# Two normalisers written with one SBUF operand, and new places for the steps of the attention's units

## The chip, the core and the metric

The kernel runs on one core of a Trainium2 chip. A core has a matrix engine (TensorE, PE in the profile; its weight loads are PEld), a vector engine (VectorE, DVE), a scalar engine (ScalarE, ACT), a general engine (GpSimd, POOL) and an engine that issues DMAs (SyncE, SP). They run side by side and wait for each other by semaphores. SBUF is the working memory, PSUM the eight banks that matrix products are written to. The metric is the time of one execution in device microseconds (us); smaller is better.

## The reference

Four layers on a 2048 x 512 array, each added to its input after a layer norm: Fourier mixing, attention with a compressive memory, and both once more.

```
a, b = x @ dft_hid_re.T, x @ dft_hid_im.T
y    = dft_seq_re @ a - dft_seq_im @ b                 # Fourier layer

for s in range(4):                                     # memory attention: segments of 512 rows, 32 heads of 16
    a_dot = softmax(qs @ ks.T / 4 + mask) @ vs         # causal, within the segment
    a_mem = (phi(qs) @ M) / (phi(qs) @ z + 1e-6)       # memory of the earlier segments
    o     = g * a_mem + (1 - g) * a_dot                # g = sigmoid(beta), one per head
    M, z  = M + phi(ks).T @ vs, z + sum(phi(ks))
out = o @ wo
```

## The kernel before

Everything is one program of four stages: Fourier, attention, Fourier, attention. Each stage consists of small generators (a projection, the scores of four heads, a memory read). A call `place(order, generator, slots)` says in which time slot each next step of a generator is written; at the end all slots are gone through in order of time, and inside a slot in order of the first number. Slots can be fractions; they are places in an order, not times. TensorE executes its matmuls in exactly this order (L118 is the helper that pins them). On the other engines a scheduler of the framework sets the order, apart from pinned instructions, so a step that is written elsewhere also moves its evictions and its DMAs.

An attention stage works through 4 segments x 4 groups of 8 heads x 2 units of 4 heads: 32 units, 10 slots each (`SU`). In the slots around a unit's start t stand:

- `stack` at t + `STK`: SP loads the unit's queries and keys as stacks (`stkq`, `stkk`, 2 DMAs each) from DRAM buffers (`scrq`, `scrk`) into which the projections were stored.
- `natural_max` at t + `N_AT`: scores in natural layout (`nat` banks, of 512, 128+384 and four times 256 columns). DVE takes each row's maximum straight from the bank (L963), and at the end writes the maxima as two-part numbers (`mparts`, L982 and L983).
- `max_rows` at t - 5: TensorE transposes them (`mT`), ACT copies them (`mt`, L998), SP writes them as extra rows into `stkq` (L1001).
- `softmax_values` at t + `S_AT`: transposed scores (`sT`), five pairs of banks: `third`, `second` twice, `first` twice. ACT applies relu on the diagonal blocks (L1034) and the exponential (`pT`, L1037); POOL zeroes what is not causal (L1040). In the last three units of the program DVE does half of the relu (L1032).
- `value_products` at t + `PV`: the products with the values (`pv_bank`, 32 matmul rows in the trace). `output` at t + `TURNED`: four transposes (`on`), the reciprocal of the row sums, times 1 - g (`rec`, L1127 and L1128), and the scaled result (L1144, L1153), which POOL adds to `onat` (L1151).

Between these stand steps that come once a group or a segment, at 2.5 slots (`W`) into a unit whose number a table gives: `mem_read` (`pm`, its normaliser `den` in L1171 to L1173, its result `onat` in L1180; table `READ_AT`), `mem_update` (`pkT`, then `pM`; `UPA` and `UPB`), `prep` (`xnT`; layer norm and transposes of the next segment; `PREP_AT`) and `transpose_out` (`oT`, split into `oh`; `OT_AT`). Every table has a variant for the first or the last segment (`_FIRST`, `_LAST`).

The rest of TensorE's time in a unit goes to a chain of projections (`pqk`, `pvv`) and output projections (`po`). `ORDER` lists 16 tiles a segment, "-" being an empty place. Each tile has 12 steps (4 blocks of 128 rows, 3 passes each); a step does the product on 64 of the 128 rows, and the other half follows `LAGS` steps later, so that two tiles run side by side on the two halves of the array. `WIN` spreads a unit's 24 steps over three stretches of its slots. All banks come from one pool of 8; a chain tile holds its bank for 12 + `LAGS` steps.

The second Fourier stage reads its rows in pairs (`normalise`, `ROWS_AT` in the new text), and its first products (`m`) are mixed into the last units of the first attention. Nothing follows the second attention; its last segment has empty places in `ORDER_LAST`.

Of the kernel before, what the change touches and what calls it, by code (L numbers as in the profile page):

```python
# [15 lines left out]
ALU = mybir.AluOpType  # L16
# [25 lines left out]
VW = DH + 1  # L42
HALF = NT // 2
URGENT = 150
S_AT = (0, 2.5, 3, 6.5, 8)
N_AT = (-17, -15.05, -12, -10.9, -8.0, -8)
PV = 11.5
PVF = 12
W = 2.5
TURN = -5  # L50
TO = 0.8
TURNED = (12.5, 12.5, 14)
WIN = ((4.1, 10), (6.1, 6), (8.1, 8))
LAGS = 17
ORDER = "k3 q3 o1 o0 o2 o3 k0 q0 k1 q1 v0 k2 v1 q2 v3 v2"
OT_AT = (1, 1, 1, 2)
PREP_AT = (2, 3)
READ_AT = (1, 3, 5, 7)
UPA = (0, 3, 5, 7)
UPB = (3, 4, 6, 8)  # L60
ORDER_FIRST = "q3 k3 - - - - v2 k0 q0 k2 k1 q1 v1 q2 v0 v3"
PREP_FIRST = (2, 3)
UPA_FIRST = (1, 3, 4, 7)
UPB_FIRST = (2, 5, 8, 8)
ORDER_LAST = "k3 q3 o2 o3 o0 - - o1 - - - - - - - -"
OT_LAST = (1, 3, 1, 1)
READ_LAST = (1, 3, 5, 5)
S_LAST = (0, 2.5, 3, 6.5, 8)
N_LAST = (-17, -15.05, -13, -11, -8, -8)
PV_LAST = 11.9  # L70
OWO = 0.8
OWU = 0.7
OWP = 0.3
OWR = 0.2
OWB = 0.55
STK = -22
TERMS = {
    "P1": (((0, 1), None, None),),
    "P7": (((1, 1), (0, 1), ALU.add),),
# [12 lines left out]
def spectral_infini_kernel(  # L92
# [649 lines left out]
    def place_attention(x_in, x_out, t0, w_at, out_at):  # L742
# [264 lines left out]
        def softmax_values(s, g, u):  # L1007
            qs, ks = stacks.pop((s, g, u, "q")), stacks.pop((s, g, u, "k"))
            K = KROWS + MROWS
            h0 = g * HG + u * HU  # L1010

            def scores(dst, *cols):
                banks = [bank("sT") for _ in SIDES]
                off, diag = 0, []
                for p, kt in cols:
                    n = 512 - kt * P
                    last = issued[0] + 1
                    for a, at in enumerate(SIDES):
                        T.matmul(
                            banks[a][:, off : off + n],  # L1020
                            ks[at : at + K, p, kt * P : (kt + 1) * P],
                            qs[at : at + K, p, kt * P :],
                            start=True,
                            stop=True,
                        )
                    diag.append(off // P)
                    off += n
                for a, ps in enumerate(banks):
                    blocks = ps.rearrange("p (b c) -> p b c", c=P)
                    blocks = blocks[:, diag[0] : diag[-1] + 1 : max(1, diag[-1] - diag[0])]  # L1030
                    if x_out is out_tiles and (s * NG + g) * NU + u >= NSEG * USEG - 3 and a:
                        V.tensor_scalar_max(blocks, blocks, 0.0)  # L1032
                    else:
                        done = A.activation(blocks, blocks, AF.Relu)  # L1034
                        if a == 0:
                            evicted.append((last, done.ins))
                    A.activation(dst[a], ps, AF.Exp, scale=-SCALE)  # L1037

            def causal(blocks):
                G.affine_select(  # L1040
                    blocks,
                    blocks,
                    pattern=[[0, n] for n in blocks.shape[1:-1]] + [[1, P]],
                    compare_op=ALU.is_ge,
                    fill=0.0,
                    base=0,
                    channel_multiplier=-1,
                )
# [12 lines left out]

            p0, p1 = [], []
            events = {}

            def ev(t, f):
                events.setdefault(t, []).append(f)

            for p in range(HP):

                def first(p=p):  # L1070
                    t = pair("pT", "wd", 8, F32)
                    p0.append(t)
                    scores((t[:, 0], t[:, 1]), (p, 0))
                    causal(t[:, :, :P])

                def second(p=p):
                    t = pair("pT", "wd", 8, F32)
                    p1.append(t)
                    scores((t[:, 0], t[:, 1]), (p, 1), (p, 3))
                    for c in 0, 3 * P:  # L1080
                        causal(t[:, :, c : c + P])

                ev((S_LAST if s == NSEG - 1 else S_AT)[3 + p], first)
                ev((S_LAST if s == NSEG - 1 else S_AT)[1 + p], second)
            p2 = []

            def third():
                t = sb.tile([P, HU, 256], F32, name="pT2", tag="craw", bufs=2)
                p2.append(t.rearrange("p (a b) s -> p a b s", b=HP))
                scores([t[:, a * HP : (a + 1) * HP].rearrange("p h s -> p (h s)") for a in range(2)], (0, 2), (1, 2))  # L1090
                causal(t[:, :, :P])

            ev((S_LAST if s == NSEG - 1 else S_AT)[0], third)

            def last():
                pb = bank("pv_bank")
                pv(pb, 0, p0, 0)
                pv(pb, 1, p1, 0)
                pv(pb, 3, p1, 384)
                pv(pb, 2, [p2[0][:, :, p] for p in range(HP)], 0)  # L1100
                ot = pair("ot", "ut", 8, F32)
                A.activation(ot[:, 0], pb, AF.Copy)
                outs[s, g, u] = ot

            pending[s, g, u] = last
            for t in sorted(events):
                for f in events[t]:
                    f()
                yield
# [7 lines left out]
        def output(s, g, u):  # L1117
# [4 lines left out]
            for i in range(LT):  # L1122
# [1 line left out]
                    pn[:, i].rearrange("p h d -> p (h d)"), ot[:, i * P : (i + 1) * P], ident  # L1124
                )
            rec = sb.tile([P, LT, HU], F32, name="rec", bufs=2)
            V.reciprocal(rec, pn[:, :, :, DH])  # L1127
            V.tensor_tensor(  # L1128
                out=rec,
                in0=rec,  # L1130
                in1=gate[:, 1:2, h0 : h0 + HU].to_broadcast([P, LT, HU]),
                op=ALU.mult,
            )
            for j in range(0, LT, 2):
                dst = o_nat[s][j // 2][:, :, h0 * DH : (h0 + HU) * DH].rearrange(
                    "p i (h d) -> p i h d", d=DH
# [19 lines left out]
        def mem_read(s, g):  # L1156
# [3 lines left out]
            for j in range(0, LT, 2):  # L1160
                pm = bank("pm", (P, 2, HG, VW))
                pms.append(pm)
                for i in range(2):
                    T.matmul(
                        pm[:, i].rearrange("p h e -> p (h e)"),
                        pq[:, (j + i) * P : (j + i + 1) * P],
                        state[g].rearrange("p h e -> p (h e)"),
                        start=True,
                        stop=True,
                    )  # L1170
                V.tensor_scalar_add(den[:, j : j + 2], pm[:, :, :, DH], 1e-6)  # L1171
            V.reciprocal(den, den)
            V.tensor_tensor(  # L1173
                out=den,
                in0=den,
                in1=gate[:, 0:1, g * HG : (g + 1) * HG].to_broadcast([P, LT, HG]),
                op=ALU.mult,
            )
            for j, pm in zip(range(0, LT, 2), pms):
                V.tensor_tensor(  # L1180
                    out=o_nat[s][j // 2][:, :, g * P : (g + 1) * P].rearrange(
# [143 lines left out]

        for n in range(NSEG * USEG):
            t = t0 + SU * n
            light_unit = n >= (NSEG - 1) * USEG
            final = n >= NSEG * USEG - 2
            place(0, softmax_values(*unit(n)), [t + k for k in sorted(set(S_LAST if light_unit else S_AT))])  # L1330
            place(0.9, value_products(*unit(n)), [t + (PVF if final else PV_LAST if light_unit else PV)])
            turned = t + TURNED[2 if n >= NSEG * USEG - 3 else n % USEG == USEG - 1]
            place(TO, output(*unit(n)), [turned])
            turn = t - (6 if x_out is out_tiles and n == NSEG * USEG - 1 else -TURN)
            place(1.9, max_rows(*unit(n)), [turn])
            place(1, natural_max(*unit(n)), [t + k for k in (N_LAST if light_unit else N_AT)])
            place(0.6, stack(*unit(n)), [t + STK])
        for s in range(NSEG):
            b = t0 + SS * s
# [77 lines left out]
    def w_at(b):  # L1417
# [7 lines left out]
    place_attention(mids[0], mids[1], b1, w_at(b1), lambda k: b1 + LB + 11 + k // 2)  # L1425
    place_spectral(
        mids[1], mids[2], a2, b2 - LEAD,
        [((2 * j, 2 * j + 1), a2 + t) for j, t in enumerate((-40, -24, -8, 2, 24, 36, 52, 66))],
        False,
    )  # L1430
    place_attention(mids[2], out_tiles, b2, w_at(b2), lambda k: b2 + LB + 8 + k)
    def setup():
        nonlocal ident, mask, same_head, gate
        with tc.issue_after(later[0].ins):
# [79 lines left out]
```

## Time and profile before

| what | value |
|---|---|
| three runs | 1796.86, 1799.59, 1799.86 us (median 1799.59) |
| the profiled execution | 1794.7 us, its span from first to last instruction 1793.0 us |
| granted TensorE clock over the span | 0.986 |
| busy: PE, PEld, DVE, ACT, POOL | 97%, 76%, 74%, 61%, 27% |

An engine's busy time is the sum of its instructions' durations without overlap. Matmuls are pipelined: the next starts while the last one's duration still runs, so a busy TensorE can be short of work, and a wait looks shorter by the part that overlaps. A releaser in square brackets is the instruction that ended a wait. The granted clock is 1.00 at full speed.

### The profile page before, as it was taken

Reading aid. Unit: us, or ns where it says so; the run is one execution under the profiler, and the core shown is the slowest. Engines: PE = TensorE matmul, PEld = TensorE weight load, DVE = VectorE, ACT = ScalarE, POOL = GpSimd, SP = SyncE. Lnnn points to the kernel's source line nnn. Section 1 sums busy time; section 2 is a strip of 40 time slices with the busy share of each in tenths; the row PEclk is TensorE's granted clock in tenths of the full one; section 3 lists DMA queues with packets and bytes.
Section 4 is the critical chain, followed back from the end, with each engine's and each line's share of the span. In section 5 each row is a group of like instructions: output and inputs, shape, how many; then the busy total and the mean of one; then the engine's idle time right before and its main releaser. Section 6 shows DMA issues by size and latency. Waiting matters only on the chain.

```text
span 1793.0 us, 35351 instructions
## 1 busy us (share of the span) xinstructions
PE 1741.7 (97%) x11504; PEld 1361.9 (76%) x11504; DVE 1324.1 (74%) x3970; ACT 1088.3 (61%) x2452; POOL 490.9 (27%) x769
## 2 busy tenths in 40 slices
PE   8999999999999999999999999999999999999998
PEld 6888777877677777777678888888876777777764
DVE  8888978864676967877877997667638677686674
ACT  3344543432688788787764675444318887877864
POOL 1000000003436465454410000000124654645432
PEclk9999999999999999999899999999999999999988
DMA  8787774355445464554556777544545546445440
GB/s 281 244 282 236 234 248 171 109 169 168 149 120 149 134 156 109 160 140 128 175 189 216 261 236 234 193 141 152 175 127 167 148 120 168 126 130 159 118 120 25
DMA packets 145511, 303.29 MB, mean 169 GB/s; under 512 B 18096, under 2 KB 22192, under 8 KB 145328
## 3 DMA queue, kind: packets, MB, share of 16 engines
q1 hardware_dynamic: 138416, 288.44, 53.6%
q10 hardware_dynamic: 6912, 12.59, 1.8%
q8 instruction: 93, 1.52, 0.4%
q14 instruction: 90, 0.74, 0.1%
HBM read 211.83 MB, written 88.08 MB: 167 GB/s over the span
## 4 chain that ended last, share of the span: by engine, by line
PE 78%; DVE 14%; issue 3%; DMA 2%; ACT 2%; SPq 0%; POOL 0%; DVEq 0%; ACTq 0%; POOLq 0%
PE m L118 24%; PE pqk L118 10%; PE pv_bank L118 8%; PE y L118 8%; PE nat L118 6%; PE pvv L118 5%; PE po L118 5%; PE u L118 4%; PE sT L118 4%; DVE junk L963 3%; DVE c L585 2%; DVE clo L135 2%; PE pM L118 1%; DMA stkk<-scrk 1%; PE on L118 1%
## 5 line engine op out<-in xcount | busy, mean ns | idle before, releaser
L963 DVE CUSTOM_DVE_ANT_0 junk<-nat,mask 128x128 bf16<-128x128 f32 (+3 forms) x896 | 369.3, 457 | 259.9 <-PE nat L118 247.1
L1037 ACT ACTIVATE pT<-sT 128x512 f32<-128x512 f32 x640 | 352.5, 609 | 2.7 <-DVE sT L1032 1.5
L118 PE MATMUL m<-chi,xa 128*128 128x512 f32 x1056 | 308.6, 392 | 2.8 <-DVE c L585 2.1
L1040 POOL TENSOR_SCALAR_AFFINE_SELECT pT<-pT 128x256 f32<-128x256 f32 (+1 forms) x448 | 193.3, 450 | 408.7 <-ACT pT L1037 290.9
L1034 ACT ACTIVATE sT<-sT 128x256 f32<-128x256 f32 x625 | 179.5, 328 | 100.4 <-PE sT L118 89.4
L118 PE MATMUL m<-clo,xa 128*128 128x512 f32 x720 | 231.8, 394 | 5.3 <-DVE clo L135 5.3
L118 PEld LDWEIGHTS m<-chi,xa 128*128 128x128 f32 x1056 | 198.2, 189 | 47.0 <-DVE c L585 2.9
L118 PE MATMUL nat<-stkk,stkq 48*128 48x384 f32 (+3 forms) x1024 | 207.8, 361 | 15.6 <-PE sT L118 3.8
L118 PE MATMUL pqk<-xT,wq 64*128 64x512 f32 (+1 forms) x720 | 189.3, 396 | 0.7 <-ACT pT L1037 0.4
L118 PEld LDWEIGHTS nat<-stkk,stkq 48*128 48x128 f32 x1024 | 128.7, 188 | 76.9 <-ACT pT L1037 15.7
L118 PE MATMUL pqk<-xT,wk 64*128 64x512 f32 (+1 forms) x720 | 186.1, 401 | 0.0
L118 PE MATMUL y<-wdt,us 128*128 128x512 f32 x768 | 182.2, 391 | 0.2 <-DVE wdt L135 0.2
L118 PE MATMUL sT<-stkq,stkk 50*128 50x256 f32 (+3 forms) x1024 | 170.3, 335 | 3.9 <-ACT pT L1037 1.4
L118 PEld LDWEIGHTS y<-wdt,us 128*128 128x128 f32 x768 | 143.4, 188 | 30.4 <-DVE wdt L135 0.9
L118 PE MATMUL pvv<-wv,xT 64*128 64x512 f32 (+1 forms) x672 | 164.4, 401 | 1.4 <-DVE onat L1153 0.8
L118 PE MATMUL pv_bank<-pT,v_all 128*32 128x384 f32 (+3 forms) x2048 | 165.4, 456 | 0.2 <-POOL pT L1040 0.2
L118 PEld LDWEIGHTS m<-clo,xa 128*128 128x128 f32 x720 | 134.8, 188 | 38.3 <-DVE clo L135 10.1
L133 ACT ACTIVATE chi<-cring 128x512 fp32r<-128x512 f32 (+1 forms) x138 | 99.7, 727 | 88.9 <-PE m L118 36.0
L204 POOL TENSOR_TENSOR r<-ve,half_neg 128x2 f32<-128x2 f32 (+2 forms) x24 | 19.7, 819 | 481.1 <-DVE ve L202 475.1
L118 PE MATMUL po<-wo,oh 64*128 64x512 f32 (+1 forms) x672 | 146.4, 402 | 0.9 <-ACT oh L133 0.5
L118 PEld LDWEIGHTS sT<-stkq,stkk 50*128 50x128 f32 x1024 | 112.4, 189 | 28.8 <-issue 8.7
L118 PEld LDWEIGHTS pqk<-xT,wq 64*128 64x128 f32 (+1 forms) x720 | 124.5, 186 | 11.1 <-issue 2.2
(189 smaller groups left out, 3157.8 us busy)
## 6 DMA issues: line engine op xcount, KB each, us to landing
cring<-in_ct SPq DMA_DIRECT2D x97, 256.0 KB
scrk<-parts SPq DMA_DIRECT2D x96, 256.0 KB
stkq<-scrq SPq DMA_DIRECT2D x128, 192.0 KB
stkk<-scrk SPq DMA_DIRECT2D x128, 192.0 KB
cring<-sum SPq DMA_DIRECT2D x95, 256.0 KB
xt<-mid SPq DMA_DIRECT2D x64, 256.0 KB
scrq<-parts SPq DMA_DIRECT2D x32, 512.0 KB
cring<-in_ct SPq DMA_DIRECT2D x27, 512.0 KB
```

The source lines that it names most:

```text
L118: return tc.keep_in_program_order(op(*args, **kwargs))
L133: pin(A.activation(hi, src, AF.Copy, scale=scale))
L135: lo_engine.tensor_tensor(out=lo, in0=src, in1=hi.bitcast(F32), op=ALU.subtract)
L204: G.tensor_tensor(out=r, in0=ve, in1=half_neg[:, :n], op=ALU.pow)
L585: V.tensor_tensor(out=dst, in0=c[tcn, base][:, m], in1=ps[m], op=op)
L963: last_max[0] = V.tensor_tensor_reduce(trash, src, mask[:, 512 - n :], 1.0, 3e38, ALU.add, ALU.min, dst,)
L1034: done = A.activation(blocks, blocks, AF.Relu)
L1037: A.activation(dst[a], ps, AF.Exp, scale=-SCALE)
L1040: G.affine_select(blocks, blocks, pattern=[[0, n] for n in blocks.shape[1:-1]] + [[1, P]], compare_op=ALU.is_ge, fill=0.0, base=0, channel ...
```

## The change

Two pieces of arithmetic. In `output` the row sums, which lie in PSUM, are first multiplied with a table and the reciprocal is taken afterwards; before it was the reciprocal first, from PSUM, and then a product of two SBUF operands. In `mem_read` one instruction with two operations adds 1e-6 and multiplies with the table, and the separate product behind the reciprocal is gone. For this the table `gate` holds 1/g and 1/(1-g) in place of g and 1-g, each bounded so that it stays finite; it is made once.

The other edits move steps. `LAGS` goes from 17 to 18. In every unit the two `first` score pairs go from slots 6.5 and 8 to 6.0 and 7.5, and `third` from 0 to 1. `READ_AT` sends group 0's memory read one unit earlier in segments 1 and 2, `UPA` and `UPB` move memory updates, `ORDER` places value tile v2 earlier. The stack loads go from 22 to 21.5 slots ahead of their unit. The `_LAST` tables now hold from the third unit of the last segment on (`SL0`; `NL0` = 1 for the natural scores) instead of the first, and differ more from the others. Five of the second Fourier stage's eight row pairs move by 2 to 10 slots.

```diff
-S_AT = (0, 2.5, 3, 6.5, 8)
-PV = 11.5
+S_AT = (1.0, 2.5, 3, 6.0, 7.5)
+PV = 11.05
-WIN = ((4.1, 10), (6.1, 6), (8.1, 8))
-LAGS = 17
+WIN = ((4.1, 9), (6.1, 7), (8.1, 8))
+LAGS = 18
-READ_AT = (1, 3, 5, 7)
+READ_AT = (0, 3, 5, 7)
-ORDER_LAST = "k3 q3 o2 o3 o0 - - o1 - - - - - - - -"
-READ_LAST = (1, 3, 5, 5)
+ORDER_LAST = "k3 q3 o2 o0 - o3 - o1 - - - - - - - -"
+READ_LAST = (1, 3, 5, 6)
-N_LAST = (-17, -15.05, -13, -11, -8, -8)
+N_LAST = (-16.5, -14.05, -13, -11.5, -10.4, -8)
-STK = -22
+STK = -21.5
+ROWS_AT = (-32, -24, -6, 2, 26, 26, 46, 66)      # was (-40, -24, -8, 2, 24, 36, 52, 66)
...
             rec = sb.tile([P, LT, HU], F32, name="rec", bufs=2)
-            V.reciprocal(rec, pn[:, :, :, DH])
             V.tensor_tensor(
                 out=rec,
-                in0=rec,
+                in0=pn[:, :, :, DH],
                 in1=gate[:, 1:2, h0 : h0 + HU].to_broadcast([P, LT, HU]),
                 op=ALU.mult,
             )
+            V.reciprocal(rec, rec)
...
-                V.tensor_scalar_add(den[:, j : j + 2], pm[:, :, :, DH], 1e-6)
+                V.scalar_tensor_tensor(
+                    den[:, j : j + 2],
+                    pm[:, :, :, DH],
+                    1e-6,
+                    gate[:, 0:1, g * HG : (g + 1) * HG].to_broadcast([P, 2, HG]),
+                    op0=ALU.add,
+                    op1=ALU.mult,
+                )
             V.reciprocal(den, den)
-            V.tensor_tensor(
-                out=den,
-                in0=den,
-                in1=gate[:, 0:1, g * HG : (g + 1) * HG].to_broadcast([P, LT, HG]),
-                op=ALU.mult,
-            )
...
-            light_unit = n >= (NSEG - 1) * USEG
+            light_unit = n >= (NSEG - 1) * USEG + SL0
+            light_nat = n >= (NSEG - 1) * USEG + NL0
...
+            V.tensor_scalar_max(gate[:, 1], gate[:, 1], 1e-30)
+            V.reciprocal(gate[:, 1], gate[:, 1])
+            V.tensor_scalar_min(gate[:, 0], eb, 1e30)
```

Three places in the order show the moves. First TensorE where the first unit's output of segment 1 is done and the rows of segment 0 are transposed for the output projection (`oT`). Before:

```order
L118 MATMUL nat<-stkk,stkq 128x256 x4
L118 MATMUL sT<-stkq,stkk 128x384 x2
L118 MATMUL sT<-stkq,stkk 128x128 x2
L118 MATMUL pm<-state_4434,phi 128x136 x4
L118 MATMUL on<-ident,ot 128x128 x4
L118 MATMUL oT<-ident,onat 128x128 x12
```

And now:

```order
L124 MATMUL nat<-stkk,stkq 128x256 x4
L124 MATMUL sT<-stkq,stkk 128x384 x2
L124 MATMUL sT<-stkq,stkk 128x128 x2
L124 MATMUL on<-ident,ot 128x128 x4
L124 MATMUL oT<-ident,onat 128x128 x12
```

The memory read `pm`, and with it its six DVE instructions, has left this stretch and stands one unit earlier.

Second, TensorE one unit later in the same segment, where the chain consists of output projections alone, from the transposed maxima (`mT`) to the last natural scores of the unit. Before:

```order
L118 MATMUL mT<-ident,mparts_71 72x64 x2
L118 MATMUL po<-wo,oh 128x512 x14
L118 MATMUL sT<-stkq,stkk 128x512 x2
L118 MATMUL po<-wo,oh 128x512 x8
L118 MATMUL sT<-stkq,stkk 128x512 x2
L118 MATMUL nat<-stkk,stkq 128x512 x2
```

And now:

```order
L124 MATMUL mT<-ident,mparts_71 72x64 x2
L124 MATMUL po<-wo,oh 128x512 x8
L124 MATMUL sT<-stkq,stkk 128x512 x2
L124 MATMUL po<-wo,oh 128x512 x12
L124 MATMUL sT<-stkq,stkk 128x512 x2
L124 MATMUL po<-wo,oh 128x512 x2
```

The first of the two score pairs stands 6 half products nearer to the maxima, and the two pairs lie 12 apart instead of 8.

Third, TensorE near the end of the program, around the value products of the third unit from the end, up to the last but one pair of transposed maxima. Before:

```order
L118 MATMUL sT<-stkq,stkk 128x256 x4
L118 MATMUL pv_bank<-pT,v_all 32x512 x4
L118 MATMUL pv_bank<-pT,v_all 32x384 x4
L118 MATMUL pv_bank<-pT,v_all 32x128 x4
L118 MATMUL pv_bank<-pT_21327,v_all 32x256 x4
L118 MATMUL nat<-stkk,stkq 128x256 x4
L118 MATMUL sT<-stkq,stkk 128x384 x2
L118 MATMUL sT<-stkq,stkk 128x128 x2
L118 MATMUL sT<-stkq,stkk 128x384 x2
L118 MATMUL sT<-stkq,stkk 128x128 x2
L118 MATMUL on<-ident,ot 128x128 x4
L118 MATMUL mT<-ident,mparts_71 72x64 x2
```

And now, without the `mT` that follows these rows:

```order
L124 MATMUL nat<-stkk,stkq 128x256 x4
L124 MATMUL sT<-stkq,stkk 128x256 x4
L124 MATMUL pv_bank<-pT,v_all 32x512 x4
L124 MATMUL pv_bank<-pT,v_all 32x384 x4
L124 MATMUL pv_bank<-pT,v_all 32x128 x4
L124 MATMUL pv_bank<-pT_21318,v_all 32x256 x4
L124 MATMUL sT<-stkq,stkk 128x384 x2
L124 MATMUL sT<-stkq,stkk 128x128 x2
L124 MATMUL pm<-state_16599,phi 128x136 x4
L124 MATMUL sT<-stkq,stkk 128x384 x2
L124 MATMUL sT<-stkq,stkk 128x128 x2
L124 MATMUL on<-ident,ot 128x128 x4
```

The last natural scores of the following unit (four of 256 columns) stand ahead of the value products instead of behind them, so their maxima are asked for earlier against the transposes `mT` that need them; one memory read has come from the unit before.

More of the change, by code (lines that the diff above doesn't have):

```diff
@@ L44 @@
 URGENT = 150
-S_AT = (0, 2.5, 3, 6.5, 8)
-N_AT = (-17, -15.05, -12, -10.9, -8.0, -8)
-PV = 11.5
+S_AT = (1.0, 2.5, 3, 6.0, 7.5)
+N_AT = (-17, -15.05, -12, -10.95, -8.0, -8)
+PV = 11.05
 PVF = 12
@@ L52 @@
 TURNED = (12.5, 12.5, 14)
-WIN = ((4.1, 10), (6.1, 6), (8.1, 8))
-LAGS = 17
-ORDER = "k3 q3 o1 o0 o2 o3 k0 q0 k1 q1 v0 k2 v1 q2 v3 v2"
+WIN = ((4.1, 9), (6.1, 7), (8.1, 8))
+LAGS = 18
+ORDER = "k3 q3 o1 o0 o2 o3 k0 q0 v2 q1 k1 k2 v1 q2 v3 v0"
 OT_AT = (1, 1, 1, 2)
 PREP_AT = (2, 3)
-READ_AT = (1, 3, 5, 7)
-UPA = (0, 3, 5, 7)
-UPB = (3, 4, 6, 8)
-ORDER_FIRST = "q3 k3 - - - - v2 k0 q0 k2 k1 q1 v1 q2 v0 v3"
+READ_AT = (0, 3, 5, 7)
+UPA = (-1, 3, 5, 7)
+UPB = (4, 4, 6, 8)
+ORDER_FIRST = "q3 k3 - - - - v2 k0 q0 k2 q1 k1 v1 q2 v3 v0"
 PREP_FIRST = (2, 3)
-UPA_FIRST = (1, 3, 4, 7)
-UPB_FIRST = (2, 5, 8, 8)
-ORDER_LAST = "k3 q3 o2 o3 o0 - - o1 - - - - - - - -"
+UPA_FIRST = (1, 2, 4, 7)
+UPB_FIRST = (2, 7, 8, 8)
+ORDER_LAST = "k3 q3 o2 o0 - o3 - o1 - - - - - - - -"
 OT_LAST = (1, 3, 1, 1)
-READ_LAST = (1, 3, 5, 5)
-S_LAST = (0, 2.5, 3, 6.5, 8)
-N_LAST = (-17, -15.05, -13, -11, -8, -8)
-PV_LAST = 11.9
+READ_LAST = (1, 3, 5, 6)
+NL0 = 1
+SL0 = 2
+TURN_LAST = -5
+TURNED_LAST = (12.5, 12.5, 14)
+TO_LAST = 1.9
+ROWS_AT = (-32, -24, -6, 2, 26, 26, 46, 66)
+S_LAST = (0.5, 2.5, 3, 6.0, 7)
+N_LAST = (-16.5, -14.05, -13, -11.5, -10.4, -8)
+PV_LAST = 10.5
 OWO = 0.8
-OWU = 0.7
+OWU = 0.6
 OWP = 0.3
 OWR = 0.2
-OWB = 0.55
-STK = -22
+OWB = 0.3
+STK = -21.5
 TERMS = {
@@ L1081, in second @@
                         causal(t[:, :, c : c + P])
-                ev((S_LAST if s == NSEG - 1 else S_AT)[3 + p], first)
-                ev((S_LAST if s == NSEG - 1 else S_AT)[1 + p], second)
+                ev((S_LAST if (s, g * NU + u) >= (NSEG - 1, SL0) else S_AT)[3 + p], first)
+                ev((S_LAST if (s, g * NU + u) >= (NSEG - 1, SL0) else S_AT)[1 + p], second)
             p2 = []
@@ L1091, in third @@
                 causal(t[:, :, :P])
-            ev((S_LAST if s == NSEG - 1 else S_AT)[0], third)
+            ev((S_LAST if (s, g * NU + u) >= (NSEG - 1, SL0) else S_AT)[0], third)
             def last():
@@ L1331, in place_attention @@
             place(0.9, value_products(*unit(n)), [t + (PVF if final else PV_LAST if light_unit else PV)])
-            turned = t + TURNED[2 if n >= NSEG * USEG - 3 else n % USEG == USEG - 1]
-            place(TO, output(*unit(n)), [turned])
-            turn = t - (6 if x_out is out_tiles and n == NSEG * USEG - 1 else -TURN)
+            turned = t + (TURNED_LAST if light_unit else TURNED)[2 if n >= NSEG * USEG - 3 else n % USEG == USEG - 1]
+            place(TO_LAST if light_unit else TO, output(*unit(n)), [turned])
+            turn = t - (6 if x_out is out_tiles and n == NSEG * USEG - 1 else -(TURN_LAST if light_nat else TURN))
             place(1.9, max_rows(*unit(n)), [turn])
-            place(1, natural_max(*unit(n)), [t + k for k in (N_LAST if light_unit else N_AT)])
+            place(1, natural_max(*unit(n)), [t + k for k in (N_LAST if light_nat else N_AT)])
             place(0.6, stack(*unit(n)), [t + STK])
@@ L1427, in spectral_infini_kernel @@
         mids[1], mids[2], a2, b2 - LEAD,
-        [((2 * j, 2 * j + 1), a2 + t) for j, t in enumerate((-40, -24, -8, 2, 24, 36, 52, 66))],
+        [((2 * j, 2 * j + 1), a2 + t) for j, t in enumerate(ROWS_AT)],
         False,
```

## The prediction

> **What bounds the kernel.** I read the page, then busy time by stage, then who TensorE waits for.
>
> ```profile
> span 1793.0 us, 35351 instructions
> PE 1741.7 (97%) x11504; PEld 1361.9 (76%) x11504; DVE 1324.1 (74%) x3970; ACT 1088.3 (61%) x2452; POOL 490.9 (27%) x769
> 455.00:905.00 450.00, 435.13 (x3799) 329.14 (x3800) 339.62 (x1377) 354.56 (x893) 223.63 (x347) 0.98 0.52 143
> 1335.00:1793.00 458.00, 439.84 (x3863) 331.26 (x3863) 319.60 (x1335) 349.21 (x878) 212.88 (x344) 0.97 0.47 125
> 1660.00:1673.20 13.20, 13.20 (x134) 10.52 (x130) 8.96 (x42) 10.25 (x27) 4.71 (x11) 1.00 0.45 120
> ```
>
> The columns after the window are its length, the busy time of PE, PEld, DVE, ACT and POOL, then granted clock, DMA share and GB/s. TensorE is the bound. The edits lie in the two attentions (second and third window row); there it is idle 14.87 + 18.16 = 33 us. The last row is one ordinary unit: 13.20 of 13.20 us busy. An ordinary unit has no wait to give back; what can be gained lies in particular units.
>
> ```profile
> PE nat L118 <- DVE onat L1180: 3.0, 7, 0.5
> PE nat L118 <- DVE mx L963: 2.6, 5, 1.3
> PE mT L118 <- DVE mparts L983: 2.4, 4, 1.2
> PE nat L118 <- DMA stkk<-scrk: 2.2, 4, 0.7
> PE sT L118 <- DVE mx L963: 1.0, 4, 0.4
> ```
>
> Each row of the waits gives total, times and the longest. They are short and spread: memory reads, maxima, stack loads. The second thing lost is clock, at the program's end:
>
> ```profile
> 1726.80:1732.50 5.70, 4.97 (x56) 2.87 (x55) 3.95 (x22) 4.87 (x13) 1.41 (x3) 1.00 0.76 146
> 1732.50:1742.80 10.30, 10.30 (x43) 7.11 (x44) 5.78 (x25) 5.22 (x15) 3.04 (x7) 0.50 0.31 66
> 1753.00:1756.40 3.40, 3.25 (x14) 1.32 (x18) 3.03 (x14) 2.31 (x5) 1.40 (x3) 0.50 0.00 0
> 1756.40:1763.20 6.80, 4.83 (x51) 2.94 (x43) 3.81 (x17) 4.35 (x12) 1.77 (x6) 1.00 0.00 0
> 1763.20:1770.10 6.90, 6.60 (x30) 3.43 (x34) 2.47 (x5) 4.65 (x12) 2.09 (x5) 0.51 0.02 5
> 1731.93 0.82 PE L118 MATMUL nat<-stkk,stkq 48*128 48x512 f32 x5 [0.68 <-DMA stkk<-scrk]
> 1760.72 0.25 PE L118 MATMUL mT<-ident,mparts 64*72 64x64 f32 x2 [1.16 <-DVE mparts L983]
> ```
>
> For 10.3 + 3.4 + 6.9 = 20.6 us the granted clock is a half; up to 10.3 us are lost so. The two long stretches each come right behind a wait: 0.68 us for a stack load, 1.16 us for maxima.
>
> **Part 1, the normalisers.**
>
> ```profile
> L1128 DVE TENSOR_TENSOR rec<-rec,gate 128x16 f32<-128x16 f32 x64 | 13.8, 216 | 1.0
> L1128 DVE TENSOR_TENSOR rec<-rec,gate x64: 161/175/656, 479.3 to 1783.8; 128x16 f32<-128x16 f32 x64
> L1171 DVE TENSOR_SCALAR den<-pm x48: 111/168/172, 584.6 to 1747.2; 128x16 f32<-128x16 f32 x48
> L1172 DVE RECIPROCAL den<-den x24: 335/344/353, 585.1 to 1748.0; 128x32 f32<-128x32 f32 x24
> L1173 DVE TENSOR_TENSOR den<-den,gate x24: 179/207/382, 585.4 to 1749.3; 128x32 f32<-128x32 f32 x24
> L983 DVE SCALAR_TENSOR_TENSOR mparts<-mx,mparts x64: 163/234/579, 452.8 to 1760.4; 128x16 fp32r<-128x16 f32 x64
> L1180 DVE TENSOR_TENSOR onat<-pm,den x48: 369/411/425, 585.9 to 1751.2; 128x256 f32<-128x256 f32 x48
>   PEld nat L118: 5.2, 8
>   PE nat L118: 3.0, 7
> 585.57 0.42 DVE L1128 TENSOR_TENSOR rec<-rec,gate 128x16 f32<-128x16 f32 x1
> 585.20 0.77 POOL L1040 TENSOR_SCALAR_AFFINE_SELECT pT<-pT 128x256 f32<-128x256 f32 x2 [2.43 <-ACT pT L1037]
> ```
>
> (The three numbers are minimum, median and maximum in ns; the two indented rows say who waited for L1180.) A memory read loses L1173, 207 ns. Its two adds become an instruction with two operations and a second operand, which the trace has only on SBUF: 168 to 234 ns, so 0 to 66 ns more each. A read is 75 to 207 ns shorter. TensorE waits for the read's end 15 times, 8.2 us in all: 15 x 0.075 to 15 x 0.207 = 1.1 to 3.1 us; I take 1.5, since the new instruction reads PSUM with 16 columns as L1171 does. The product in `output` now reads PSUM and one SBUF operand. L1128 is stretched where a POOL select runs (0.42 us at 585.57, against a minimum of 0.161): 64 x (216 - 161) = 3.5 us of DVE, on the path only where TensorE soon waits for DVE, which is the six units with `oT`. There 0.25 us each are 1.5; I take 1.0, bounds 0 and 3.5. Part 1: -2.5, from -6.6 to 0. The new reciprocals cost what the old ones did; making the table costs three small instructions once, ahead of the attention, under the products of the first Fourier stage.
>
> **Part 2, the memory read out of the `oT` unit** (first place in the order).
>
> ```profile
>   PEld po L118: 2.6, 6
>   PEld nat L118: 2.3, 6
> ```
>
> These rows of the tile `oh` say that weight loads wait 4.9 us for the split of `oT`, in six units. DVE does a whole read ahead of it: 2 x 168 + 344 + 207 + 2 x 411 = 1709 ns, more than the 0.8 us of waiting a unit. Four of the six units lose the read: up to -4 x 0.8 = -3.3. In its new unit the read will be waited for as elsewhere, 8.2 us / 15 = 0.55 each: +2.2. Sum -1.1, from -3.3 to +2.2.
>
> **Part 3, the maxima in the last segment** (third place). The four 256-column scores now stand ahead of the value products, so `mparts` is done long before `mT`. Of the 2.4 us above, 1.16 is the row quoted and 0.7 more falls into the first attention's last units:
>
> ```profile
> PE mT L118 <- DVE mparts L983: 0.7, 1, 0.7
> PE nat L118 <- DMA stkk<-scrk: 0.5, 1, 0.5
> ```
>
> Both go: -1.9 (0 if another DVE step slips in ahead of them). **Part 4, stack loads.** They can start when the last `sT` pair of three units earlier has read the stack. In the last segment that pair now stands ahead of a `nat` pair and of more output projections, about 0.8 us (some four matmuls) sooner, and more chain work follows it. The 0.68 and 0.5 waits go, with their overlapped parts -1.5; bounds -2.2 (the whole row) and 0.
>
> **Part 5, the clock.** Without the 1.16 us wait the window ahead of 1763.2 is fuller, and I count that stretch gone: 6.9 / 2 = -3.4. Bounds: -10.3 (all three) and +3.4 (another such stretch). [...]
>
> **Part 6, all the rest**, at 0: the score steps of ordinary units, `LAGS`, memory updates, ROWS_AT. What hides them is the 13.20 of 13.20 row: these steps are done while the chain runs. If that cover is gone, an eviction wait costs 1.0 / 4 = 0.25 us in a unit. I allow -3 to +3. SP's queue: the maxima's rows now stand ahead of some stores of projections; nobody in the waits above waits for those stores.
>
> The sum: -2.5 - 1.1 - 1.9 - 1.5 - 3.4 = -10.4 us, on the profiled execution 1794.7 - 10.4 = 1784.3. That execution is 4.9 us under the median of the runs, 1799.59; against the median the forecast is 1789.
>
> **The rivals.**
>
> [...]
>
> *All three half-speed stretches go*: -7.0 - 10.3 = -17.3, 1782. Against it: the last two units of the program have no chain tile at all.
>
> *Nothing moves*: each wait only changes its place, above all the memory reads of part 2 (+2.2) and the stack loads. Within 0.2% of the median (3.6 us, about what a measurement of this kernel can tell from no change), some 1799.
>
> *Slower, by PSUM banks.* The second place in the order: the first score pair comes 8 half products after `mT`, not 14, and a chain tile holds its bank 30 steps instead of 29 (12 + `LAGS`). So the pair asks for banks that DVE still reads for maxima. The trace has this wait: 1.0 us in 4 times for `sT` and 2.6 in 5 for `nat`, 0.25 to 0.52 each. Some 44 units have a full chain; at 0.4 in each, 44 x 0.4 = 17.6, less the 10.4 gained: 1807. It decides from 14.0 / 0.4 = 35 units on (10.4 + 3.6). Against it: such waits are rare now, though two score pairs and `nat` share the banks already.
>
> **How the numbers follow.** Forecast (parts 1 to 5) 0.38; clock unchanged 0.20; all clock back 0.12; nothing 0.17; slower 0.13. The third place of the order is the surest, and it carries parts 3 and 5, so the forecast is first. Faster by over 0.2%: 0.38 + 0.20 + 0.12 less 0.03 for the edge of the clock-unchanged case = 0.67; same 0.17 + 0.02 = 0.19; slower 0.13 + 0.01 = 0.14. The range takes parts 1 to 6 at their better ends only in part, down to 1775 (the full-clock case and 7 us of parts 1, 2 and 6), and up to 1804, which leaves out most of the slower case. The forecast's own range is 1783 to 1796.
>
> **What would show it.** Right: L1173's place empty and the new two-operation instruction under 0.2 us; no `mT` wait for `mparts` over 0.3 us in the last segment; the `oh` waits under 2 us; fewer than 20 us at half clock behind 1726. Wrong: `sT` waiting for L963 or L1037 in ordinary units (banks); a new row of `nat` waiting for L1180 one unit ahead of each `oT`; half-speed stretches in the middle of the attention.

## The result, and the profile after

| | before | changed |
|---|---|---|
| median of four runs | 1798.22 us | 1777.43 us |
| ratio, 95% interval | | 0.9890 [0.9859, 0.9920] |
| the profiled execution | 1794.7 us | 1775.0 us |

The change gains 20.8 us, twice the forecast 10.4. It was timed again later beside the kernel before, on the chip of the third group of experiments: 1776.44 against 1795.40 us, ratio 0.9898 [0.9874, 0.9922], a gain of 19.0.

First two lines of the page of the changed kernel:

```profile
span 1773.2 us, 35306 instructions
PE 1723.8 (97%) x11504; PEld 1341.4 (76%) x11504; DVE 1314.6 (74%) x3949; ACT 1095.5 (62%) x2452; POOL 489.5 (28%) x769
```

Then its busy time by stage (columns as before). The last row is the end of the program, from the fifth value products from the end on; the fence after it holds the same stretch of the kernel before.

```profile
455.00:897.00 442.00, 428.61 (x3794) 319.61 (x3796) 334.07 (x1366) 358.62 (x893) 221.66 (x347) 0.98 0.55 146
1327.00:1773.20 446.20, 427.80 (x3865) 319.66 (x3864) 315.99 (x1323) 352.79 (x878) 213.48 (x344) 0.99 0.49 129
1717.95:1773.20 55.25, 47.92 (x371) 30.57 (x370) 34.38 (x133) 33.49 (x82) 15.32 (x36) 0.95 0.21 54
```

```profile
1726.80:1793.00 66.20, 57.40 (x375) 35.85 (x374) 34.29 (x139) 34.50 (x82) 15.34 (x36) 0.85 0.19 46
```

TensorE is the bound as before. Of the 19.8 us between the two spans, 8.0 lie in the first attention (450.0 to 442.0) and 10.95 in the last five units. There 20.5 us at half clock became 3.4 (and 4.7 behind the last matmul, where the clock costs nothing): (20.5 - 3.4) / 2 = 8.5 us. The other 2.4 us were won at full clock; TensorE's idle time there fell by 1.5 us (66.20 - 57.40 against 55.25 - 47.92).

The instructions of the normalisers (minimum, median and maximum in ns):

```profile
L1133 DVE TENSOR_TENSOR rec<-on,gate x64: 110/165/176, 479.4 to 1762.8; 128x16 f32<-128x16 f32 x64
L1139 DVE RECIPROCAL rec<-rec x64: 239/253/255, 480.0 to 1763.0; 128x16 f32<-128x16 f32 x64
L1177 DVE SCALAR_TENSOR_TENSOR den<-pm,gate x48: 156/169/175, 571.5 to 1742.7; 128x16 f32<-128x16 f32 x48
L1185 DVE RECIPROCAL den<-den x24: 337/345/353, 572.0 to 1742.9; 128x32 f32<-128x32 f32 x24
```

The product is never stretched any more (maximum 176 ns, before 656), and the instruction with two operations costs 169 ns, as much as the one with one operation (168). So VectorE saves 24 x 207 ns = 5.0 us for the removed product and 64 x (216 - 165) ns = 3.3 us of stretching.

Who TensorE waits for in the changed kernel, and then who waits for the split `oh`:

```profile
PE sT L124 <- DMA stkq<-mt: 2.7, 1, 2.7
PE nat L124 <- DMA stkk<-scrk: 2.1, 2, 1.6
PE sT L124 <- DVE mx L969: 2.0, 5, 0.7
PE mT L124 <- DVE mparts L989: 0.6, 2, 0.3
PE nat L124 <- DVE onat L1187: 0.4, 2, 0.2
```

```profile
  PEld nat L124: 3.8, 6
  PEld po L124: 2.1, 6
  PE nat L124: 1.9, 4
```

Waits for memory reads fell from 3.0 to 0.4 us and for `mparts` from 2.4 to 0.6. Waits for stack loads stayed (2.2 to 2.1), and one of 2.7 for the extra rows is new. Both differ from one execution to the next: a second profile of the changed kernel (`after_again`, below) has 0.8 us for stack loads and no wait for the extra rows. The waits of `sT` for the maxima rose from 1.0 to 2.0 us; 1.4 of the 2.0 lie in two units that the experiments come back to.

### The profile page after: what moved, and what is told of

Its sections match the earlier page's. It is cut to its first block, busy times and chain, and to the rows that moved or that the text cites. A ratio compares the mean times of both kernels' runs of the same rounds, so it can differ in the third digit from the quotient of the medians.

```text
span 1773.2 us, 35306 instructions
## 1 busy us (share of the span) xinstructions
PE 1723.8 (97%) x11504; PEld 1341.4 (76%) x11504; DVE 1314.6 (74%) x3949; ACT 1095.5 (62%) x2452; POOL 489.5 (28%) x769
## 4 chain that ended last, share of the span: by engine, by line
PE 78%; DVE 12%; ACT 4%; issue 3%; DMA 2%; POOL 0%; SPq 0%; DVEq 0%; ACTq 0%; POOLq 0%
PE m L124 26%; PE pqk L124 9%; PE y L124 8%; PE pv_bank L124 8%; PE nat L124 5%; PE u L124 5%; PE pvv L124 5%; PE po L124 4%; PE sT L124 4%; DVE junk L969 2%; DVE c L591 2%; DVE clo L141 1%; ACT pT L1043 1%; PE pM L124 1%; PE on L124 1%
## 5 line engine op out<-in xcount | busy, mean ns | idle before, releaser
L969 DVE CUSTOM_DVE_ANT_0 junk<-nat,mask 128x128 bf16<-128x128 f32 (+3 forms) x896 | 368.9, 457 | 231.6 <-PE nat L124 217.4
L124 PE MATMUL nat<-stkk,stkq 48*128 48x384 f32 (+3 forms) x1024 | 197.3, 354 | 12.3 <-PE sT L124 3.4
L124 PE MATMUL pqk<-xT,wq 64*128 64x512 f32 (+1 forms) x720 | 193.7, 399 | 0.8 <-ACT pT L1043 0.6
L124 PE MATMUL pvv<-wv,xT 64*128 64x512 f32 (+1 forms) x672 | 173.2, 402 | 0.5 <-DVE xT L141 0.4
L124 PEld LDWEIGHTS nat<-stkk,stkq 48*128 48x128 f32 x1024 | 122.6, 187 | 65.8 <-ACT pT L1043 19.3
L124 PE MATMUL sT<-stkq,stkk 50*128 50x256 f32 (+3 forms) x1024 | 165.6, 334 | 5.9 <-DMA stkq<-mt 2.7
L124 PE MATMUL pv_bank<-pT,v_all 128*32 128x512 f32 (+3 forms) x2048 | 162.5, 452 | 0.2 <-DVE xr L235 0.2
L210 POOL TENSOR_TENSOR r<-ve,half_neg 128x2 f32<-128x2 f32 (+2 forms) x24 | 19.7, 819 | 481.3 <-DVE ve L208 457.5
L124 PEld LDWEIGHTS sT<-stkq,stkk 50*128 50x128 f32 x1024 | 105.5, 188 | 37.3 <-issue 12.4
```

Of the source, the lines that this page charges most:

```text
L124: return tc.keep_in_program_order(op(*args, **kwargs))
L210: G.tensor_tensor(out=r, in0=ve, in1=half_neg[:, :n], op=ALU.pow)
L969: last_max[0] = V.tensor_tensor_reduce(trash, src, mask[:, 512 - n :], 1.0, 3e38, ALU.add, ALU.min, dst,)
```

## The experiments

Each run lists its span and its mean granted clock. Their product is my estimate of the time that the span would have had at full clock; what is left of the span went to the half clock. Averages of both over the runs, as differences to the kernel before in the same group, tell work and waits from clock. From the scatter of the runs, a figure at full clock is good to 1 to 1.6 us and one of the half clock to 2 to 4 us (95%); a difference of two rows is good to about 2 us at full clock and 3 to 5 us at half. And up to 2 us of the clock's loss lie behind the last matmul, where it costs nothing: by up to so much the gain at full clock is overstated, and that of the half clock understated. The kernel before had a product of 1764.2, 1765.6 and 1764.3 us in the three groups and lost about 30 us to the clock each time.

| kernel | median, before | ratio to before, 95% | at full clock | half clock |
|---|---|---|---|---|
| norm_only | 1802.69, 1795.64 | 1.0040 [1.0024, 1.0056] | +2.9 | +4.3 |
| tail_only | 1782.38, 1795.64 | 0.9923 [0.9899, 0.9946] | -6.9 | -7.6 |
| mid_only | 1804.34, 1795.64 | 1.0045 [1.0029, 1.0060] | +1.1 | +6.7 |
| read_back | 1782.84, 1795.64 | 0.9930 [0.9903, 0.9957] | -7.7 | -5.5 |
| no_norm | 1781.53, 1797.35 | 0.9913 [0.9895, 0.9931] | -8.3 | -7.9 |
| nlast_back | 1778.85, 1797.35 | 0.9896 [0.9874, 0.9917] | -10.6 | -8.5 |
| order_back | 1776.05, 1797.35 | 0.9885 [0.9865, 0.9906] | -11.3 | -10.3 |
| before_fill | 1798.42, 1797.35 | 0.9993 [0.9976, 1.0010] | +7.1 | -8.3 |
| after_again | 1776.44, 1795.40 | 0.9898 [0.9874, 0.9922] | -11.8 | -7.2 |
| norm_fix | 1793.39, 1795.40 | 0.9988 [0.9972, 1.0005] | -1.5 | -0.1 |
| after_fill | 1784.79, 1795.40 | 0.9944 [0.9923, 0.9965] | -2.2 | -8.5 |
| slast_back | 1780.96, 1795.40 | 0.9925 [0.9900, 0.9950] | -9.3 | -4.1 |

The change itself is `after_again`: 11.8 us of work and waits, 7.2 us of clock.

### One part alone: norm_only, tail_only, mid_only

`norm_only` is the kernel before with the changed code of the normalisers and of the table `gate`. `tail_only` has the `_LAST` tables and the lines that read them; `mid_only` has all other numbers (several lines are written as one):

```diff
 # tail_only
+NL0 = 1; SL0 = 2; TO_LAST = 1.9
+S_LAST = (0.5, 2.5, 3, 6.0, 7); N_LAST = (-16.5, -14.05, -13, -11.5, -10.4, -8); PV_LAST = 10.5
+ORDER_LAST = "k3 q3 o2 o0 - o3 - o1 - - - - - - - -"; READ_LAST = (1, 3, 5, 6)
...
 # mid_only
+S_AT = (1.0, 2.5, 3, 6.0, 7.5); PV = 11.05; WIN = ((4.1, 9), (6.1, 7), (8.1, 8)); LAGS = 18
+READ_AT = (0, 3, 5, 7); STK = -21.5; ROWS_AT = (-32, -24, -6, 2, 26, 26, 46, 66)
...
```

> The kernel before with the new normalisers alone, all steps at their old places. Theory T (the gain lies in the last segment's places, some -12 of the -20.8 us, and the normalisers bring what their working gave): -2.5 us, between -1 and -5. Rival N (relief of the vector engine everywhere: its normaliser time fell by about 9 us in the two profiles, and late maxima or memory reads are behind many of the short waits): -8 to -12. Rival 0 (normalisers only pay together with the new places): within 1 us of no change.

> The kernel before with the tables of the last segment alone (the _LAST tables, from its second and third unit on). Theory T: -10 to -14 us, with fewer than 12 us at half clock behind 1720 and the last five units together some 11 us shorter. Rival N: -3 to -5, since the waits of the last units would end late without a relieved vector engine. As the prediction had it (its parts 3, 4 and 5): -6.8.

> The kernel before with the steps of the ordinary units, memory steps, stack loads, the order of the chain tiles and the row pairs at their new places; the last segment's tables and the normalisers as before. Theory T: -3 to -5 us (what is left of -20.8 after -12 and -2.5 to -4), most of it in the first attention, where the unit with a half-speed stretch at 633 lost 2 us. As the prediction had it (parts 2 and 6): -1.1, between -6 and +5. Rival N: 0 to +2, the places alone bring nothing.

`tail_only` came as theory T had it (-13.3 us by the medians, and the half clock behind 1720 fell to 6.8 us and 2.0 behind the last matmul). The other two came as no theory had them: each alone makes the kernel slower, by 7.1 and 8.7 us. The parts would add up to +2.5, the change gives -19.0.

For `norm_only` the place is plain. It is the unit of the 17th value products of each attention, a unit with `oT`; here the second attention's, first in the kernel before, then in norm_only, where the second row is the stretch at half clock in it:

```profile
1572.63:1588.90 16.27, 15.27 (x139) 11.98 (x138) 13.65 (x54) 13.37 (x33) 8.46 (x13) 1.00 0.37 98
```

```profile
1575.90:1595.98 20.08, 16.63 (x139) 12.47 (x138) 14.39 (x56) 14.29 (x34) 9.43 (x14) 0.92 0.34 87
1590.90:1594.31 3.41, 3.41 (x20) 2.65 (x18) 1.42 (x7) 1.61 (x5) 1.21 (x2) 0.50 0.18 55
```

The wait that norm_only has more, and its rows in the order of time:

```profile
PE po L118 <- DVE mx L963: 4.8, 2, 2.4
```

```profile
1586.57 0.17 DVE L202 TENSOR_SCALAR ve<-row_mv 128x2 f32<-128x2 f32 x1
1587.58 1.22 DVE L209 TENSOR_TENSOR rt<-r 128x2 f32<-128x2 f32 x1 [0.84 <-POOL r L204]
1589.62 0.28 DVE L963 CUSTOM_DVE_ANT_0 junk<-nat,mask 128x128 bf16<-128x128 f32 x1
1590.44 0.50 PE L118 MATMUL po<-wo,oh 64*128 64x512 f32 x1 [2.40 <-DVE mx L963]
```

With shorter normalisers the scheduler put a layer norm's step L209 (at 1587.58) ahead of four row maxima (L963), the first of them the third row (at 1589.62); in the kernel before it stands behind them (at 1585.47, the maxima from 1583.47 on). L209 needs a power that GpSimd computes (`r`, L204), so VectorE stood for 0.84 us and was slow after it (L209 took 1.22 us, 0.57 in the kernel before), the maxima held their bank, and TensorE waited 2.40 us for it. Behind that came 3.41 us at half clock. The two attentions lose 2 x 3.8 us in this unit and 2 x 1.2 in the next.

`mid_only` has the same order in the same unit of both attentions, with the old normalisers (L209 is L210 here, L963 is L964). TensorE waits 1.64 us for the maxima there, 0 in the kernel before:

```profile
709.29 0.16 DVE L210 TENSOR_TENSOR rt<-r 128x2 f32<-128x2 f32 x1 [0.85 <-POOL r L205]
711.39 0.28 DVE L964 CUSTOM_DVE_ANT_0 junk<-nat,mask 128x128 bf16<-128x128 f32 x1
712.21 0.49 PE L119 MATMUL sT<-stkq,stkk 50*128 50x512 f32 x1 [1.64 <-DVE mx L964]
```

So other places of the steps are enough to bring this order about. The first attention has another new loss, a `nat` wait of 1.0 us for a memory read at 848, with 13.65 us at half clock behind it. The end of the program, on the old tables, lost 13.7 us to the clock ahead of the last matmul in its profile (10.2 before). The wait at 848, and its stretch:

```profile
PE nat L119 <- DVE onat L1181: 1.0, 1, 1.0
```

```profile
846.00:862.70 16.70, 15.64 (x77) 10.03 (x77) 10.78 (x38) 8.44 (x22) 8.65 (x14) 0.59 0.62 160
```

### The normalisers put right, and taken out: norm_fix, no_norm

```diff
 # norm_fix: norm_only with
-                row_scale(rr, ve, r)
+                with behind_max():
+                    row_scale(rr, ve, r)
```

> norm_only with one line more: the layer norm's four small steps (row_scale in prep) may be issued on the vector engine only behind the row maxima written before them. Theory S (alone, the new normalisers lost 2.4 us of waiting for a bank and 1.7 us by the half clock behind it in one unit of each attention, since these steps went ahead of four maxima): the waits of 2.4 us go, and with them 7 to 10 us against norm_only; ratio to before 0.996 to 0.999, since what is left is the saving of the shorter normalisers, 2 to 5 us. Rival (the new instructions themselves cost more than the old): as norm_only, ratio 1.003 to 1.005.

> The changed kernel with the old normalisers; every step at its new place. Theory S (alone, the new normalisers made the scheduler of the vector engine put a layer norm's steps ahead of four row maxima, and TensorE waited 2.4 us for a bank in one unit of each attention; with the new places that does not happen, and the shorter normalisers give what they save): 2 to 5 us slower than the changed kernel, ratio to before 0.990 to 0.993. Rival A (the parts add up; norm_only was +7, tail_only -13.5, mid_only +8.7): the new normalisers cost 7 us here too, so this kernel is faster than the changed one, ratio to before 0.985. Rival C (only the half-speed stretches differ): clocked at full speed both take the same, within 1 us.

With the layer norm's steps held behind the maxima, the wait of `po` for `mx` is gone, the unit takes 16.48 us at full clock, and the kernel is 9.3 us faster than `norm_only` by the medians:

```profile
1571.59:1588.07 16.48, 15.12 (x139) 11.85 (x138) 13.95 (x54) 13.63 (x33) 8.40 (x13) 1.00 0.39 101
```

So theory S is right about `norm_only`: the order of VectorE took what the normalisers save, and more. What they save alone is small, 1.5 us at full clock, and the ratio to before, 0.9988 [0.9972, 1.0005], is not clear of no change. In the changed kernel they are worth the difference of `no_norm` and `after_again`, 11.8 - 8.3 = 3.5 us at full clock, as theory S had it. But its reason is wrong: the order does come about in the changed kernel, in the same unit of both attentions (L209 is L215 now, L963 is L969):

```profile
705.58 0.16 DVE L215 TENSOR_TENSOR rt<-r 128x2 f32<-128x2 f32 x1 [0.85 <-POOL r L210]
705.85 0.28 DVE L969 CUSTOM_DVE_ANT_0 junk<-nat,mask 128x128 bf16<-128x128 f32 x1
707.87 0.50 PE L124 MATMUL sT<-stkq,stkk 50*128 50x512 f32 x1 [0.70 <-DVE mx L969]
```

VectorE stands for 0.85 us ahead of the first of the four maxima, and TensorE waits 0.70 us. With the old normalisers (`no_norm`) it waits 1.6 us there in the first attention and 1.1 in the second, and the unit is 1.4 and 0.9 us longer. That is 2.3 of the 3.5 us. No run held the layer norm's steps behind the maxima in the changed kernel, so what that would bring is not known.

### The memory read back in the unit of oT: read_back

```diff
-READ_AT = (0, 3, 5, 7)
+READ_AT = (1, 3, 5, 7)
```

> The changed kernel with group 0's memory read back in the unit of oT (READ_AT = (1, 3, 5, 7)). If the prediction's part 2 holds: +1.1 us against the changed kernel, between -2 and +3.3, and 0.8 us more waiting for oh in each of four units. Theory T, by the waits of the two profiles (weight loads waited 5.9 us for oh after, 4.9 before): no effect, within 1 us.

```profile
  PEld nat L124: 4.0, 8
  PEld po L124: 2.5, 6
```

```profile
PE nat L124 <- DMA stkk<-scrk: 1.6, 1, 1.6
PE nat L124 <- ACT pT L1043: 1.2, 1, 1.2
```

(The first two rows say who waits for the tile `oh`, the others are TensorE's waits from 1484 to 1503.) Against the changed kernel it loses 4.1 us at full clock, good to 2 us, more than either theory said. But weight loads wait 6.5 us for `oh`, against 5.9 with the read one unit earlier: the mechanism of part 2 is not there. In the profile 2.7 us are lost in one unit, from 1484, by the two waits shown; the same unit of the first attention has none of it. In the units that the read left or entered, gains and losses (-1.0, +0.8; -1.0, +0.5, +0.4, +0.6) nearly cancel. What the move is worth stays open between 0 and 4 us.

### The last segment taken apart: nlast_back, order_back, slast_back

```diff
 # each from the changed kernel
+N_LAST = (-16.5, -14.05, -13, -11.5, -8.0, -8)            # nlast_back
+ORDER_LAST = "k3 q3 o2 o3 o0 - - o1 - - - - - - - -"      # order_back
+S_LAST = (0, 2.5, 3, 6.5, 8)                              # slast_back
```

> The changed kernel with the fifth number of N_LAST back at -8.0: in the last segment the four natural scores of 256 columns stand behind the value products again. Prediction's part 3: +1.9 us of waits for mparts in mT, and part 5: about +3.4 us by one more half-speed stretch, together +5. Rival: the maxima are early enough by the other moves (the earlier score pairs and value products), then within 1 us.

> The changed kernel with the old ORDER_LAST: output projections in the third and fourth empty place again (two tiles in the fourth and fifth, none in the sixth). Theory T (the last units gained since work and waits lie better): +3 to +6 us, and the units from 1718 on longer. Rival: this table only moves the same products from one unit to the next, within 1 us.

> The changed kernel with the old score slots in the last segments (S_LAST = (0, 2.5, 3, 6.5, 8)); maxima, value products and output projections at their new places. Theory T (the units 26 and 61, counted from the first value products, gained 1.6 and 2.2 us since the first two score pairs come sooner behind the maxima and the exponential is done when the value products ask): +3 to +5 us against the changed kernel. Rival M (what these two units gained comes from the maxima ahead of the value products): within 1 us.

`nlast_back` is as fast as the change by the ratios (0.9896 and 0.9898 to before), as the rival had it and not the +5 of the prediction. It loses 1.2 us at full clock, which is within the noise, and nothing at half clock (-8.5 against -7.2). In its profile the third unit from the end is 1.0 us longer at full clock, and `mT` waits 0.8 there, but behind an exponential and no longer behind `mparts`:

```profile
PE mT L124 <- ACT pT L1043: 0.8, 1, 0.8
PE oT L124 <- POOL onat L1157: 0.6, 1, 0.6
```

So the profile shows a wait of part 3's kind, at most half as large as forecast, the runs cannot tell it from nothing, and no half-speed stretch shows in them beside it. `order_back` is as fast as the change: the new places of the output projections bring nothing that the runs can tell. `slast_back` is slower than `after_again`, which ran with it, by a ratio of 1.0031 [1.0008, 1.0054], 5.5 us by the means, about what theory T had, but not where T looked: the two units named are unchanged, and of the 5.5 about 2.5 are at full clock and 3 at half. The other tables of the last segment (the places of the value products and outputs, and from which unit on the tables hold) were not taken apart.

### The clock by itself: before_fill, after_fill

```diff
+            w = ws["q" if s == 0 else "o", 0]
+            for _ in range(FILL.get((int(x_out is out_tiles), n, kind), 0)):
+                T.matmul(ps, w[:, 0, :P], w[:, 0], start=True, stop=True)
```

> The kernel before with 24 additional matmuls of 128 rows and 512 columns (weights times weights) in the last four units but one, each written to a score bank or a bank of transposed maxima ahead of the products that overwrite it, where TensorE waited or had only products on 48 or 50 rows. [...] Rival W (the clock falls after a wait, whatever its length has to be): the waits for transfers and maxima stay, so the stretches stay, and the time is 2 to 6 us longer. [...]

(21 of the 24 are in the program; three named a bank that does not occur.) The end of the program, from the same value products on as in the row of before shown above:

```profile
1736.41:1799.40 62.99, 57.35 (x396) 34.26 (x395) 34.23 (x139) 34.40 (x82) 15.31 (x36) 0.97 0.20 48
1771.40:1774.80 3.40, 3.40 (x16) 2.52 (x15) 1.59 (x4) 3.40 (x9) 1.07 (x3) 0.50 0.05 10
```

The clock there rises from 0.85 to 0.97, and of 20.5 us at half clock one stretch of 3.4 is left (and 2.8 behind the last matmul): the end is 3.2 us shorter although it does more work. Over the runs the half clock costs 8.3 us less, and the work 7.1 us more, 0.34 us a matmul. The kernel as a whole is where it was. The rival had the stretches unchanged, and two of the three went; the price, 7.1 us, is about what the clock gave back, 8.3. Some of the added products filled waits, so this run alone does not separate "little work" from "a wait"; the count in the last section tells more.

> The changed kernel with 38 additional matmuls of 128 rows and 512 columns (weights times weights, overwritten by the products that follow in the same bank), placed where TensorE waits or works on 48 or 50 rows in the first and last units of the attentions. [...] Rival W (the clock follows waits): stretches stay, 5 us slower.

```profile
1361.00:1372.00 11.00, 10.48 (x89) 7.28 (x78) 9.79 (x38) 10.56 (x29) 6.50 (x9) 1.00 0.68 217
1378.80:1382.20 3.40, 2.60 (x16) 1.83 (x17) 3.27 (x10) 2.49 (x8) 0.95 (x3) 1.00 0.01 4
1382.20:1389.03 6.83, 6.83 (x27) 5.29 (x26) 2.75 (x11) 3.47 (x9) 0.81 (x2) 0.50 0.45 101
```

In three places where work was added the clock stays full (the stretch at 1367.8 is gone, as are those at 497 and 870), but one stands at 846 although work was added there, and behind 497 and 1367.8 the next thin place, one unit on, is hit instead (508 and 1382). It loses 9.6 us at full clock against the change and wins 1.3 at half clock: a ratio of 1.0046 [1.0027, 1.0066] to `after_again`. Here the padding costs more than the clock pays.

## Why the prediction was right, and too small

The time lies in the range (1775 to 1804) and on the side foretold, but it is below the forecast's own range (1783 to 1796). That the wide range holds it is in part luck: its lower end was made of the full clock and 7 us of parts 1, 2 and 6, and what came beside the clock were mainly parts 3 and 4. The sum was half of what came: 7.0 us of work and waits forecast, 11.8 measured (10 to 12, by the caution above); 3.4 of clock forecast, 7.2 measured (7 to 9).

- **Part 1 (-2.5).** Measured -3.5 in the changed kernel, -1.5 alone, each good to 1 to 2 us. The prices held at their good ends (169 ns; no stretching), and TensorE's waits for reads fell by 2.6. What it lacked is the scheduler: VectorE's shorter instructions change which one is put next, and that cost 10 us in `norm_only`. The new places change it too: in the changed kernel the layer norm's step also stands ahead of the four maxima, and TensorE waits 0.70 us there in each attention. No term of the forecast has this wait.
- **Part 2 (-1.1).** The step that failed: the waits for `oh` did not fall below 2 us; weight loads wait 5.9 us, before 4.9. DVE was not late for `oh` because of the read.
- **Part 3 (-1.9).** No `mT` wait for `mparts` over 0.3 is left. But going back in this place alone costs nothing that the runs can tell (`nlast_back`, 1.2 us at full clock, good to 2), so the other moves of the last segment also bring the maxima early enough.
- **Part 4 (-1.5).** No stack load is waited for behind 1717 any more, nor around 830, but the sum over the program is the same (2.1): one of 1.6 stands in an ordinary unit of the second attention (0.8 there in `after_again`, which has no other). "What is late next" was not asked for the ordinary units, whose loads also start half a slot later.
- **Parts 3 and 4 as a sum** are the term that was mis-sized: 3.4 forecast, 6.9 by `tail_only`; in its profile the last segment of the first attention is 3.8 us shorter at full clock and that of the second 3.3. The forecast took only the rows of `mparts` and `stkk`. These are the waits of the kernel before in its fourth unit from the end, which has no chain tile behind it:

```profile
PE nat L118 <- ACT pT L1037: 0.3, 1, 0.3
PE sT L118 <- ACT pT L1037: 0.3, 1, 0.3
PE nat L118 <- DVE mx L963: 0.3, 1, 0.3
PE sT L118 <- ACT mt L998: 0.3, 1, 0.3
PE pv_bank L118 <- POOL pT L1040: 0.2, 1, 0.2
```

They add up to 1.4 us, none of them is left in the changed kernel, and that unit is 2.2 us shorter at full clock. In the first attention the unit at 827, with the 0.7 and 0.5 us of the forecast's rows, gains 1.6. The tables hold in both attentions, and the forecast priced mostly one.

- **Part 5 (-3.4).** Measured -7.2, and -7.6 by the last segment's tables alone. Not one of three half-speed stretches went but two and most of the third: 20.5 us became 3.4 (and 4.7 behind the last matmul, which cost nothing). The forecast tied the one that it counted gone to the 1.16 us wait ahead of it; no run shows that tie. By the count of the last section the 3.41 us ahead of the three had little work, 2304, 1668 and 1120.
- **Part 6 (0).** `mid_only` gives +1.1 at full clock, within its bounds; that it costs 6.7 us of clock on the old last segment was not foreseen. The reason given for the 0, one ordinary unit with 13.20 of 13.20 us busy, does not hold for the others. These are the two middle segments of the first attention, before and changed:

```profile
580.43:812.12 231.69, 224.64 (x2109) 176.69 (x2108) 178.00 (x733) 182.04 (x457) 120.81 (x190) 0.99 0.53 139
```

```profile
581.79:807.15 225.36, 220.18 (x2106) 168.11 (x2104) 173.52 (x724) 184.61 (x457) 121.38 (x190) 1.00 0.55 143
```

With the 1.7 us that 3.4 us at half clock cost in the first row taken out, they are 4.6 us shorter, of which the normalisers alone (`norm_fix`) bring 0.9. Those of the second attention are 2.0 us shorter, and the first segments of both 0.8 and 2.3 us longer; the second profile of the changed kernel agrees within 1 us.

- **The rivals.** The nearest is "all three half-speed gone" (-17.3). The slower one, by banks, did not come: `sT` waits 2.0 us in 5 times for maxima (1.0 in 4 before), nowhere near 44 units; 1.4 of the 2.0 are the two waits behind the layer norm's step.

`norm_fix`, `tail_only` and `mid_only` add up to -7.3 us at full clock, the change gives -11.8. The difference of 4.5 is good to about 3 us. The profiles place 3.2 of it in the unit of the 17th value products: in each attention it is 0.2 us longer than before in `norm_fix` and 1.0 longer in `mid_only`, unchanged in `tail_only`, but 0.4 shorter in the changed kernel. The rest stays open.

## What to carry to other kernels

Read the clock of each part of a run beside its time: span times granted clock tells work from clock. For the kernel before it has a standard deviation of 1.2 to 1.7 us, the time itself 3.2 to 3.5. When an instruction gets cheaper under a scheduler, compare the order of its engine, not only its durations: one small step that waits for another engine, put ahead of four that release banks, cost more than the saving. Look for it in the kernel that you keep as well: here it is still there, with 0.70 us. And price the end of a program by all its small waits; with no filler work behind them they all count.

## What the hardware showed that was not expected

Many half-speed stretches came without a long wait ahead of them. The shortest are 3.41 us long (`norm_only`, 1590.90 to 1594.31). I cut all fourteen profiles into windows of that length which begin where the stretches begin, and added up, for each window at full clock, columns times rows over 128 of the matmuls that started in it:

```
work of one window (columns at 128 rows)  next window at half clock  at full clock
below 2000                                         65                      2
2000 to 3400                                       50                    253
3400 and more                                       3                   6689
```

A dense window of the Fourier stages has 7680. Idle time tells less: of the windows with a wait of 1 us or more, 28 were followed by half clock and 34 were not, and 13 of the 118 changes to half clock came behind a window whose longest idle time was under 0.2 us. But none of the 118 came behind a window without any idle time (the least is 0.19 us in sum), and no run changed the work alone. So these are counts in the traces of this kernel and its variants; what sets the clock is not shown. One of the 13, in the changed kernel, and one in the kernel before:

```profile
1733.09:1736.50 3.41, 2.98 (x17) 1.83 (x16) 3.41 (x15) 3.14 (x10) 1.67 (x5) 0.99 0.02 5
1736.50:1739.91 3.41, 3.41 (x19) 1.48 (x23) 3.20 (x16) 1.80 (x4) 0.79 (x2) 0.51 0.00 0
```

```profile
858.70:862.10 3.40, 3.10 (x18) 2.14 (x18) 3.40 (x19) 2.15 (x7) 2.37 (x6) 1.00 0.26 95
862.10:868.93 6.83, 6.83 (x31) 4.52 (x33) 4.50 (x18) 4.60 (x12) 1.54 (x4) 0.50 0.47 99
```

TensorE was busy for 2.98 of 3.41 and 3.10 of 3.40 us, but with products on 48, 50 and 64 of 128 rows: by the count these two windows have 2192 and 3024. Most of this kernel's spread goes with the clock: over the runs of before in the three groups (23, 17 and 19), span and granted clock have correlations of -0.87, -0.89 and -0.95.
